# Retention attention before two expert layers: state products as 64x64 blocks, and half of the masked scores left out in tiles 4 to 11

## The chip, the cores and the metric

The kernel runs on one core of one Trainium2 chip. The metric is the device time of one execution in microseconds, as the median of several runs. A core has a matrix engine (PE, TensorE, 128 rows by 128 columns; the profile shows the loads of its weights apart as PEld), a vector engine (DVE), a scalar engine (ACT), a general engine (POOL), and queues that issue transfers (SP above all). Matmuls write into PSUM, eight banks of 128 partitions by 512 floats, which DVE and ACT read.

## The reference, cut to what matters

For each of 2 batches and 8 heads, 768 tokens of 64 features go through a decaying linear attention; its output (1536 tokens of 512 features) goes through two layers of the same form.

```
state = gamma * state + k[t] outer v[t]            # per head, 64x64
y[t] = scale * q[t] @ state
x = y as (1536, 512)
layer(x, w_in, w_out, f) = f(x @ w_in) @ w_out     # 512 -> 2048 -> 512
out = layer(layer(x, ..., elu), ..., softplus)
```

## The kernel before

The tokens are cut into 12 tiles of 128, six of a batch. Within a tile the attention is done in chunked form. With q scaled by a power of gamma and v by its inverse, a tile's output is (q times the state at the tile's start) plus (the masked 128x128 scores times v); the state then takes in the tile's k and v. All of this is float32. The layers work on blocks of 512 tokens (4 tiles) in 16 units of 128 hidden features, 96 units in all; each factor is split into a rounded part and a rest, so that each product is made of three passes.

The order of everything is a list of steps, `OPENING`, followed by what `regular()` makes of the rest; a step's name is followed by the tile's or unit's number, and each engine takes its own instructions in the order of the list. The steps that matter here:

- `Lq`, `Lk`, `Lv`, `Lw`: transfers of a tile's q, k, v and of a piece of the weights, all issued by SP.
- `dq`, `dv`: scaling of q (DVE, tiles 0 and 1) and of v (POOL). `kc.n`: n matmuls on zeros, which write nothing that is used.
- `Tq`, `Tk`: q and k turned to features by tokens, two heads at a time (L241, four matmuls); `tq` (DVE) and `tk` (ACT) copy them out. Tiles 9 to 11 are turned on DVE instead.
- `S`: scores (L300), eight matmuls with 64 rows; the two heads of a pair use the upper and the lower 64 rows and write to two banks. `m`: the mask, two operations of DVE (L310).
- `ST`, `st`: the tile's contribution to the state (L280, eight matmuls with 64 output columns, 64 wide), added and scaled on DVE.
- `sp`: POOL copies the states of two heads into the two diagonal 64x64 blocks of a 128x128 tile `wide`, whose other blocks hold zeros (L271).
- `O`: the output (`attend`). If the tile isn't a batch's first, `wide` times q for two heads at once (L322, four matmuls); then v times the masked scores (L328, eight matmuls with 128 rows and 64 output columns). `xh` (ACT) and `xl` (DVE) split the result for the layers.
- `ca`, `cb`, `ih`, `il`, `oh`, `ol`: conversion and splitting of weights. `H`, `aa`, `ab`, `gh`, `gl`, `R`, `F`: a unit's first product (L356, 12 matmuls), activation, splitting, second product (L418, 12 matmuls) and end of a block.

A float32 matmul of `S`, `ST` or `O` stands as two matmuls in the trace: the four of L322 are x8 there, the eight of L328, L300 and L280 are x16. A transpose and a matmul of the layers stand as one.

Of the kernel before, what the change touches and what calls it, by code (L numbers as in the profile page):

```python
# [37 lines left out]
def tile_retention_elu_softplus(  # L38
# [43 lines left out]
    def load(n, j):  # L82
# [24 lines left out]
    dec = const.tile([P, 2 * H + HP], F32, name="dec")  # L107
    gq = const.tile([P, HP * P], F32, name="gq")
    nc.scalar.dma_start(out=dec, in_=decay)
    gv = dec[:, 0:H].unsqueeze(2).to_broadcast([P, H, D])  # L110
    gt = dec[:, H + HP:].unsqueeze(2).to_broadcast([P, H, D])
# [9 lines left out]
                            compare_op=ALU.is_ge, fill=0.0)  # L121
    one = ones[:, 0:1]
# [5 lines left out]
    wb = ps.tile([P, 512], F32, tag="a3", name="wb")  # L128

    def keep_clock(n):  # L130
        for _ in range(n):
            nc.tensor.matmul(wb, warm[:, 0:P], warm, start=True, stop=True)  # L132
# [74 lines left out]
    def psum(tag):  # L207
        return ps.tile([P, 512], F32, tag=tag, name=tag)


    banks = ["h0", "h1", "a0", "a1", "a2", "r0", "r1"]
    turn = [0]

    def few_banks():
        banks[:] = ["r0", "r1"]
        turn[0] = 0

    def rbank():
        turn[0] += 1
        return psum(banks[(turn[0] - 1) % len(banks)])  # L220

    wide = [const.tile([P, HP, P], F32, name=f"wide{i}") for i in range(2)]
    for w in wide:
        nc.gpsimd.memset(w, 0.0)
# [399 lines left out]
```

## Time and profile before

| | |
|---|---|
| median of 3 runs | 587.7 us (587.6 to 587.92) |
| the profiled execution | 587.7 us, of which the span from its first to its last instruction is 586.0 us |
| busy: PE | 580.2 us (99%), 3012 matmuls |
| busy: DVE, ACT, POOL | 465.5, 413.3 and 30.2 us |
| granted TensorE clock | 1.0 throughout |

The time of the execution is 1.7 us more than the span; what is worked out on the span is carried over with that. Busy shares are of the whole span; a matmul's recorded duration is longer than the distance to the next one, since matmuls overlap, so the rate of PE is read from starts, not from durations.

### The profile page before, as it was taken

To read this page: it belongs to the slowest core of one execution; us is meant where nothing else is said; L and a number is where in the kernel's file an instruction comes from. 1 tells how busy PE (TensorE), PEld (TensorE's weight loads), DVE (VectorE), ACT (ScalarE), POOL (GpSimd) and SP (SyncE) were. 2 spreads that over 40 slices of the span, in tenths; PEclk is the share of its full clock that TensorE was granted. 3 is DMA by queue.
4 is the path that set the end of the run, shared out by engine and by line. 5 is a ranking of instruction groups with operands and counts; after the bars stand their busy time and mean duration, and the time that the engine had idled before them with its cause. 6 is when DMAs were issued, how large, how long until landed. Compare 5 with 4: busy or idle time off the path is not lost.

```text
span 586.0 us, 8280 instructions
## 1 busy us (share of the span) xinstructions
PE 580.2 (99%) x3012; PEld 478.3 (82%) x3012; DVE 465.5 (79%) x746; ACT 413.3 (71%) x696; POOL 30.2 (5%) x45
## 2 busy tenths in 40 slices
PE   8999999999999999999999999999999999999997
PEld 5888888888888888888888888888888888888886
DVE  4999899975664456898898998788878778878775
ACT  2688887945454557889889777767766766766763
POOL 3202010121020000000000000000000000000000
PEclk9999999999999999999999999999999999999999
DMA  9977676634310001365553000000100000100001
GB/s 222 320 202 240 205 199 201 188 103 92 66 19 1 1 0 54 101 205 157 167 179 109 0 2 0 1 0 2 72 1 0 1 0 2 72 2 1 0 1 72
DMA packets 71705, 47.74 MB, mean 81 GB/s; under 512 B 49520, under 2 KB 65904, under 8 KB 71664
## 3 DMA queue, kind: packets, MB, share of 16 engines
q1 hardware_dynamic: 71376, 46.94, 27.7%
q8 instruction: 24, 0.39, 0.3%
q10 hardware_dynamic: 288, 0.27, 0.1%
q14 instruction: 17, 0.14, 0.1%
HBM read 44.05 MB, written 3.15 MB: 81 GB/s over the span
## 4 chain that ended last, share of the span: by engine, by line
PE 98%; DMA 1%; ACT 0%; DVE 0%; issue 0%
PE h L356 45%; PE a L418 38%; PE r L418 7%; PE r L300 2%; PE r L328 2%; PE r L322 1%; PE r L280 1%; PE r L241 1%; DMA xl<-q 1%; PE h L241 0%; PE a L241 0%; PE a L300 0%; PE a L328 0%; PE a L322 0%; PE wb L132 0%; ACT kT L260 0%
## 5 line engine op out<-in xcount | busy, mean ns | idle before, releaser
L356 PE MATMUL h<-xh,wh 128*128 128x512 f32 x384 | 103.2, 391 | 0.0
L356 PE MATMUL h<-xh,wl 128*128 128x512 f32 x384 | 102.7, 389 | 0.0
L356 PE MATMUL h<-xl,wh 128*128 128x512 f32 x384 | 102.7, 389 | 0.0
L356 PEld LDWEIGHTS h<-xl,wh 128*128 128x128 f32 x384 | 72.1, 188 | 15.0
L356 PEld LDWEIGHTS h<-xh,wl 128*128 128x128 f32 x384 | 72.1, 188 | 15.1
L356 PEld LDWEIGHTS h<-xh,wh 128*128 128x128 f32 x384 | 71.7, 188 | 15.1 <-issue 0.3
L196 DVE TENSOR_TENSOR wl<-wo,wh 128x512 fp32r<-128x512 f32 x96 | 66.9, 697 | 18.4 <-ACT wh L190 18.3
L190 ACT ACTIVATE wh<-wo 128x512 fp32r<-128x512 f32 x96 | 60.3, 629 | 27.9 <-PE a L418 24.7
L196 DVE TENSOR_TENSOR wl<-wi,wh 128x512 fp32r<-128x512 f32 x96 | 66.5, 693 | 0.3 <-ACT wh L190 0.2
L190 ACT ACTIVATE wh<-wi 128x512 fp32r<-128x512 f32 x96 | 59.5, 620 | 0.7 <-DVE wi L183 0.7
L418 PE MATMUL a<-gh,wh 128*128 128x512 f32 x192 | 56.2, 399 | 0.0
L418 PE MATMUL a<-gh,wl 128*128 128x512 f32 x192 | 54.4, 390 | 0.0
L418 PE MATMUL a<-gl,wh 128*128 128x512 f32 x192 | 54.3, 389 | 0.0
L391 ACT ACTIVATE gh<-w 128x512 fp32r<-128x512 f32 x48 | 30.3, 632 | 33.9 <-DVE w L386 33.9
L370 ACT ACTIVATE e<-h 128x512 f32<-128x512 f32 x48 | 28.6, 596 | 31.7 <-PE h L356 31.7
L365 ACT ACTIVATE e<-h 128x512 f32<-128x512 f32 x48 | 28.6, 596 | 30.0 <-PE h L356 29.1
L383 DVE TENSOR_SCALAR w<-e 128x512 f32<-128x512 f32 x48 | 20.5, 426 | 36.5 <-ACT e L371 36.4
L170 ACT ACTIVATE cl<-raw,half 128x512 int32<-128x512 uint32 x64 | 48.4, 756 | 0.1
L379 DVE SCALAR_TENSOR_TENSOR e<-e,h 128x512 f32<-128x512 f32 x48 | 32.7, 680 | 18.5 <-ACT e L366 18.5
L182 DVE SCALAR_TENSOR_TENSOR cl<-cm,cl 128x512 int32<-128x512 int32 x64 | 44.9, 702 | 1.8 <-ACT cl L170 1.8
L169 ACT ACTIVATE cm<-raw 128x512 f32<-128x512 f32 x64 | 42.4, 663 | 3.2 <-DMA raw<-moe_w_out 1.5
L418 PEld LDWEIGHTS a<-gh,wl 128*128 128x128 f32 x192 | 36.1, 188 | 7.7
(124 smaller groups left out, 916.1 us busy)
## 6 DMA issues: line engine op xcount, KB each, us to landing
raw<-moe_w_in SPq DMA_DIRECT2D x32, 512.0 KB, 3.9
raw<-moe_w_out SPq DMA_DIRECT2D x32, 512.0 KB, 3.7
out_dram<-o SPq DMA_DIRECT2D x11, 256.0 KB, 2.0
k<-k SPq DMA_DIRECT2D x8, 256.0 KB, 4.3
v<-v SPq DMA_DIRECT2D x8, 256.0 KB, 4.9
q<-q SPq DMA_DIRECT2D x5, 256.0 KB, 6.0
xl<-q SPq DMA_DIRECT2D x4, 256.0 KB, 4.1
xh<-k SPq DMA_DIRECT2D x4, 256.0 KB, 3.9
```

What stands on the lines that cost most here:

```text
L169: nc.scalar.activation(out=m, in_=r[:, :, :, 1].bitcast(F32), func=AF.Copy, scale=2.0 ** -112)
L170: nc.scalar.activation(out=l, in_=r[:, :, :, 0].bitcast(U32), func=AF.Relu, scale=2.0 ** -29, bias=half)
L182: nc.vector.scalar_tensor_tensor(out=l, in0=m.bitcast(I32), scalar=3, in1=l, op0=ALU.logical_shift_left, op1=ALU.bitwise_or)
L190: nc.scalar.activation(out=h, in_=wf[f][o], func=AF.Copy)
L196: nc.vector.tensor_tensor(out=l, in0=wf[f][o], in1=ws[u, o][0].bitcast(F32), op=ALU.subtract)
L356: nc.tensor.matmul(b, w[:, kk, :], x[:, kk, :], start=(n == 0), stop=(n == len(seq) - 1))
L365: nc.scalar.activation(out=e, in_=h, func=AF.Relu, scale=-1.0)
L370: nc.scalar.activation(out=e, in_=h, func=AF.Abs)
L379: nc.vector.scalar_tensor_tensor(out=e, in0=e, scalar=-1.0, in1=h, op0=ALU.add, op1=ALU.max)
L383: nc.vector.tensor_scalar(out=w, in0=e, scalar1=1.0, scalar2=-1.0, op0=ALU.add, op1=ALU.add)
L391: nc.scalar.activation(out=gh, in_=acts[u][0], func=AF.Copy)
L418: nc.tensor.matmul(acc[i], st[:, i * P:(i + 1) * P], mv, start=(fresh and p == 0), stop=(f == NF - 1 and p == 2))
```

## The change

In `attend` the product with the state is no longer made with `wide` for two heads at once. Each head's 64x64 state is a weight block of its own, and four heads stand in the four 64x64 quadrants of the matrix engine: eight matmuls in place of four. The head's place (upper or lower 64 rows) is now `h // 4` instead of `h % 2`, and the output has its head `h % 2` in the output partitions and `h // 4` in the bank, so it takes two neighbouring banks. `sp`, `wide` and their copies go away.

In tiles 4 to 11 (`turned_tiles`) v times the masked scores is done in two parts: the first 64 queries with the first 64 values alone (64 rows, 64 output columns, 64 wide), and the last 64 queries with all 128 values (128 rows, 64 wide). To have the first 64 values of the second four heads in the lower partitions, the two halves of their tokens are exchanged when k and v are loaded, with a mask `mask_t` to match.

The eight banks of PSUM are one tile, `psb`; a bank is picked by a list in order of use, scores and outputs take pairs, and a state may take a free bank of `h`. Loads of q and k from tile 1 on are cut into two transfers, those of k and v of tiles 4 to 11 into three. `OPENING` is written anew: it is longer (up to unit 14 of the first layer), and its start has another order of loads and transposes.

```diff
-Lq.0 Lk.1 Lk.0 Lq.1 dq.0 Lv.0 Tq.0 kc.3 Lk.2 Lq.2 Tk.0 kc.2 Lv.1 Tk.1 dq.1 tk.1 Lg.0 tq.0 Tq.1 Lv.2 tk.0 dv.0 tq.1 S.0
+Lq.0 Lk.1 Lq.1 Lk.0 dq.0 Lq.2 Tq.0 kc.3 Lv.0 dq.1 Lv.1 tq.0 Lk.2 Tk.0 Tq.1 tk.0 Lq.3 tq.1 S.0 Lg.0 Lk.3 Tk.1 dv.0 m.0
+Tq.2 tk.1 Lv.2 ST.0 dv.1 Lk.4 O.0 S.1 Lw.0 xh.0 Lv.3 xl.0 kc.2 st.0 Lq.4 ST.1 m.1 Tk.2 Lw.1 tk.2 Lw.3 tq.2 O.1 Lw.2
...
-        nc.sync.dma_start(out=t, in_=src[b, :, c * P:(c + 1) * P, :].rearrange("h s d -> s h d"))
+        src = src[b, :, c * P:(c + 1) * P, :].rearrange("h s d -> s h d")
+        if n and j in turned_tiles:
+            lo, hi = (t[:, 0::2, :], t[:, 1::2, :]) if n == 1 else (t[:, :HP, :], t[:, HP:, :])
+            nc.sync.dma_start(out=lo, in_=src[:, :HP, :])
+            nc.sync.dma_start(out=hi[D:], in_=src[:D, HP:, :])
+            nc.sync.dma_start(out=hi[:D], in_=src[D:, HP:, :])
+        elif n == 2 or j == 0:
+            nc.sync.dma_start(out=t, in_=src)
+        else:
+            for i in range(2):
+                nc.sync.dma_start(out=t[:, i::2, :], in_=src[:, i * HP:(i + 1) * HP, :])
...
-    def spread_state(j):
-        if j % CPB and j < NTILE:
-            for i in range(2):
-                r = slice(i * D, (i + 1) * D)
-                nc.gpsimd.tensor_copy(wide[j % 2][r, :, r], states[j][r])
...
-        b = bank["s", j] = rbank()
...
+        free = [n for n in range(2) if n not in hbanks.values()]
+        bank["s", j] = (free[0], psb[:, free[0]]) if hbanks and free else rbank()
...
-        b = bank["o", j] = rbank()
-        first = True
-        if j % CPB:
-            s = wide[j % 2]
-            for pr in range(HP):
-                nc.tensor.matmul(b[:, pr * P:(pr + 1) * P], s[:, pr, :], qT[:, pr, :], start=(pr == 0), stop=False,
-                                 skip_group_check=True)
-            first = False
-        for pr in range(HP):
-            for i in range(2):
-                o = i * D
-                nc.tensor.matmul(b[o:o + D, pr * P:(pr + 1) * P], vt[:, 2 * pr + i, :], a[i][:, pr, :],
-                                 start=(first and pr == 0), stop=(pr == HP - 1), skip_group_check=True)
...
+        bank["o", j] = rbank(2)
+        b = bank["o", j][1]
+        inter = j % CPB > 0
+        if inter:
+            for pr in range(0, HP, 2):
+                for i in range(2):
+                    for e in range(2):
+                        r = slice(i * D, (i + 1) * D)
+                        nc.tensor.matmul(b[e * D:(e + 1) * D, i, pr * D:pr * D + P], states[j][r, pr + e, :], qT[r, pr + e, :],
+                                         start=(pr == 0), stop=False, skip_group_check=True)
+        if j in turned_tiles:
+            for o in range(0, HP, 2):
+                for i in range(2):
+                    for e in range(2):
+                        r = slice(i * D, (i + 1) * D)
+                        nc.tensor.matmul(b[e * D:(e + 1) * D, i, o * D:o * D + D], vt[r, i * HP + o + e, :], a[i][r, o + e, 0:D],
+                                         start=(not inter and o == 0), stop=False, skip_group_check=True)
+            for o in range(0, HP, 2):
+                for i in range(2):
+                    for e in range(2):
+                        nc.tensor.matmul(b[e * D:(e + 1) * D, i, o * D + D:o * D + P], vt[:, i * HP + o + e, :], a[i][:, o + e, D:P],
+                                         start=False, stop=(o > 0), skip_group_check=True)
+            return
...
```

Three places show what moves. The first is PE around the output of tile 7, between a unit's products; a row is one line's matmuls that follow each other, L322 and L328 are the output, L280 the state. Before:

```order
L356 MATMUL h_1263<-xh_293,wl 128x512 x4
L322 MATMUL r_1280<-qT,wide_146 128x128 x4
L328 MATMUL r_1280<-A,v 64x128 x8
L280 MATMUL r_1295<-v,k 64x64 x8
L418 MATMUL a_630<-gh,wh 128x512
```

In the change the same tile's output stands after the second product of a unit; L369 is the product with the states, L376 and L381 are the two parts of the masked scores, L323 is the state:

```order
L485 MATMUL psb<-gl,wh 128x512 x4
L369 MATMUL psb<-qT,st 64x128 x8
L376 MATMUL psb<-A,v 64x64 x8
L381 MATMUL psb<-A,v 64x64 x8
L323 MATMUL psb<-v,k 64x64 x8
L485 MATMUL psb<-gh,wh 128x512 x4
```

Twelve matmuls of width 128 became eight of width 128 and sixteen of width 64, in three shapes instead of two.

The second place is PE's start, from the transpose of tile 0's k on, where L132 (L155) are the matmuls on zeros. Before:

```order
L241 MATMUL h_165<-ident,xh_89 128x128 x4
L132 LDWEIGHTS warm
L132 MATMUL wb<-warm 128x512
L132 LDWEIGHTS warm
L132 MATMUL wb<-warm 128x512
L241 MATMUL a_173<-ident,xh_89 128x128 x4
L241 MATMUL a_184<-ident,xl_88 128x128 x4
L300 MATMUL a_195<-qT,kT 128x128
```

In the change (L281 are the transposes, of k with `xh`, of q with `xl`; L344 the scores, L323 the state, L388 the output of tile 0):

```order
L281 MATMUL psb<-ident,xh_89 128x128 x4
L281 MATMUL psb<-ident,xl_88 128x128 x4
L344 MATMUL psb<-qT,kT 128x128 x8
L281 MATMUL psb<-ident,xh_89 128x128 x4
L281 MATMUL psb<-ident,xl_88 128x128 x4
L323 MATMUL psb<-xl_90,xh_89 64x64 x8
L388 MATMUL psb<-A,xl_90 64x128 x8
L344 MATMUL psb<-qT,kT 128x128 x8
L155 LDWEIGHTS warm
L155 MATMUL psb<-warm 128x512
```

The transpose of k of tile 1 and two matmuls on zeros moved from ahead of the first scores to behind them.

The third place is DVE between the mask of tile 4 and the splitting that the first unit's second product (`R.0`) reads, in the change; L205 and L206 convert weights, L219 splits them, L445 is the activation and L462 its splitting:

```order
L354 TENSOR_TENSOR A<-psb,mask 128x512 x2
L205 SCALAR_TENSOR_TENSOR cl<-cm,cl 128x512
L206 SCALAR_TENSOR_TENSOR wo_117<-raw,cl 128x512
L445 SCALAR_TENSOR_TENSOR e<-e,psb 128x512
L205 SCALAR_TENSOR_TENSOR cl<-cm,cl 128x512
L206 SCALAR_TENSOR_TENSOR wi_122<-raw,cl 128x512
L219 TENSOR_TENSOR wl<-wi_120,wh 128x512
L205 SCALAR_TENSOR_TENSOR cl<-cm,cl 128x512
L206 SCALAR_TENSOR_TENSOR wo_119<-raw,cl 128x512
L219 TENSOR_TENSOR wl<-wo_117,wh 128x512
L462 TENSOR_TENSOR gl<-e,gh 128x512
```

Before, 18 operations stood in this place, and PE made the first products of units 2 and 3 ahead of a second product; now it makes that of unit 2 alone.

## Rows read from the trace of the kernel before

**Rows 1.** Page: busy us of each engine; granted clock in 40 slices, tenths.
```profile
PE 580.2 (99%) x3012; PEld 478.3 (82%) x3012; DVE 465.5 (79%) x746; ACT 413.3 (71%) x696; POOL 30.2 (5%) x45
...
PEclk9999999999999999999999999999999999999999
```
**Rows 2.** Page, the chain that ended last: share of the span by engine.
```profile
PE 98%; DMA 1%; ACT 0%; DVE 0%; issue 0%
```
**Rows 3.** Timeline of PE, tile 7: start us, us, line, tiles, shape, count.
```profile
95.14 1.07 PE L356 MATMUL h<-xh,wh 128*128 128x512 f32 x4
...
97.86 1.05 PE L322 MATMUL r<-qT,wide 128*128 128x128 f32 x8
98.84 1.09 PE L328 MATMUL r<-A,v 128*64 128x128 f32 x16
99.77 0.63 PE L280 MATMUL r<-v,k 128*64 128x64 f32 x16
100.33 1.20 PE L418 MATMUL a<-gh,wh 128*128 128x512 f32 x4
...
103.21 1.07 PE L356 MATMUL h<-xh,wh 128*128 128x512 f32 x4
```
**Rows 4.** One line's operations (L322, L328, L280): ns min/median/max, first and last start.
```profile
L322 PE MATMUL r<-qT,wide x56: 270/275/275, 33.1 to 180.6; 128*128 128x128 f32 x56
L328 PE MATMUL r<-A,v x128: 272/273/324, 34.1 to 181.6; 128*64 128x128 f32 x128
L280 PE MATMUL r<-v,k x96: 219/222/271, 41.2 to 161.9; 128*64 128x64 f32 x96
```
**Rows 5.** Timeline of PE: scores of tiles 0 and 3, matmul by matmul.
```profile
9.19 0.27 PE L300 MATMUL a<-qT,kT 64*128 64x128 f32 x1
9.19 0.27 PE L300 MATMUL r<-qT,kT 64*128 64x128 f32 x1
9.30 0.27 PE L300 MATMUL a<-qT,kT 64*128 64x128 f32 x1
...
19.93 0.27 PE L300 MATMUL h<-xh 64*128 64x128 f32 x1
19.96 0.27 PE L300 MATMUL r<-xh 64*128 64x128 f32 x1
20.04 0.27 PE L300 MATMUL h<-xh 64*128 64x128 f32 x1
```
**Rows 6.** Timeline of PE, the start, up to the first scores.
```profile
6.77 0.59 PE L132 MATMUL wb<-warm 128*128 128x512 bf16 x2
7.20 0.60 PE L241 MATMUL a<-ident,xh 128*128 128x128 f32 x4
7.64 0.66 PE L241 MATMUL a<-ident,xl 128*128 128x128 f32 x4
8.97 0.37 PE L300 MATMUL a<-qT,kT 64*128 64x128 f32 x1 [0.68 <-ACT kT L260]
```
**Rows 7.** Timelines of ACT (L260) and DVE, the same stretch.
```profile
7.84 0.60 ACT L260 ACTIVATE kT<-a 128x512 f32<-128x512 f32 x1 [5.75 <-PE a L241]
8.33 0.59 ACT L260 ACTIVATE kT<-h 128x512 f32<-128x512 f32 x1
...
6.89 0.69 DVE L231 TENSOR_TENSOR xl<-xl,dec 128x512 f32<-128x512 f32 x1 [2.41 <-DMA xl<-q]
```
**Rows 8.** Windows: busy us of each engine (count), clock, DMA share, GB/s.
```profile
25.80:58.00 32.20, 32.20 (x195) 26.22 (x194) 30.94 (x49) 28.22 (x49) 4.94 (x5) 1.00 0.78 234
58.00:98.00 40.00, 40.00 (x246) 32.79 (x245) 37.68 (x61) 35.74 (x63) 2.64 (x3) 1.00 0.71 211
```
**Rows 9.** Timeline of DVE, weights converted and split, one after the other.
```profile
23.58 0.68 DVE L182 SCALAR_TENSOR_TENSOR cl<-cm,cl 128x512 int32<-128x512 int32 x1
24.29 0.69 DVE L183 SCALAR_TENSOR_TENSOR wi<-raw,cl 128x512 int32<-128x512 int32 x1
24.90 0.68 DVE L339 TENSOR_TENSOR xl<-h,xh 128x512 fp32r<-128x512 f32 x1
25.50 0.68 DVE L196 TENSOR_TENSOR wl<-wi,wh 128x512 fp32r<-128x512 f32 x1
```

More of the change, by code (lines that the diff above doesn't have):

```diff
@@ L121, in tile_retention_elu_softplus @@
                             compare_op=ALU.is_ge, fill=0.0)
+    mask_t = const.tile([P, P], F32, name="mask_t")
+    for i in range(2):
+        nc.gpsimd.affine_select(out=mask_t[i * D:(i + 1) * D], in_=ones[i * D:(i + 1) * D], pattern=[[1, P]], base=(i - 1) * D,
+                                channel_multiplier=-1, compare_op=ALU.is_ge, fill=0.0)
     one = ones[:, 0:1]
@@ L127, in tile_retention_elu_softplus @@
     nc.vector.memset(warm, 0.0)
[L128 removed]
+    psb = ps.tile([P, 8, 512], F32, name="psb")
+    names = ("h0", "h1", "a0", "a1", "a2", "a3", "r0", "r1")
     def keep_clock(n):
         for _ in range(n):
[L132 removed]
+            nc.tensor.matmul(psb[:, 5], warm[:, 0:P], warm, start=True, stop=True)
     keep_clock(7)
@@ L207, in psum, with rbank, keep, release @@
     def psum(tag):
[L208 to L224, printed above, removed]
+        n = names.index(tag)
+        assert n not in live
+        return psb[:, n]
+    banks = [2, 3, 4, 6, 7, 0, 1, 5]
+    live = set()
+    def rbank(n=1):
+        free = [b for b in banks if b not in live]
+        if n == 2:
+            b = min((p for p in (0, 2, 4, 6) if p in free and p + 1 in free), key=lambda p: max(free.index(p), free.index(p + 1)))
+        else:
+            b = free[0]
+        for i in range(b, b + n):
+            banks.remove(i)
+            banks.append(i)
+            live.add(i)
+        return b, psb[:, b] if n == 1 else psb[:, b:b + 2]
+    def keep(n):
+        keep_clock(n)
+        banks.remove(5)
+        banks.append(5)
+    def release(key):
+        b, t = bank.pop(key)
+        live.discard(b)
+        if key[0] in "ao":
+            live.discard(b + 1)
+        return t
     qkT = {}
@@ L309, in causal @@
         for i in range(2):
-            nc.vector.tensor_tensor(out=a[i], in0=bs[i].rearrange("p (h t) -> p h t", h=HP),
-                                    in1=mask.unsqueeze(1).to_broadcast([P, HP, P]), op=ALU.mult)
+            nc.vector.tensor_tensor(out=a[i], in0=bs[:, i].rearrange("p (h t) -> p h t", h=HP),
+                                    in1=(mask_t if i and j in turned_tiles else mask).unsqueeze(1).to_broadcast([P, HP, P]), op=ALU.mult)
         scores[j] = a
@@ new lines, in attend, with turned, feature @@
+        for n in range(H):
+            i, pr = (n % 2, n // 2) if j == 0 else divmod(n, HP)
+            h = head(j, i, pr)
+            e, o = h % 2, h % HP // 2 * P
+            nc.tensor.matmul(b[e * D:(e + 1) * D, h // HP, o:o + P], vt[:, h, :], a[i][:, pr, :], start=(not inter and h % HP < 2),
+                             stop=(h % HP >= 2), skip_group_check=True)
+    def turned(b):
+        return b[:, :, 0:2 * P].rearrange("p i (a t) -> p i a t", a=2)
+    def feature(x, j):
+        return x[:, :, (j % TPB) * P:(j % TPB + 1) * P].rearrange("p (i a) t -> p i a t", i=2)
@@ L352, in hidden @@
         b = psum(f"h{u % 2}")
+        banks[:] = [n for n in banks if n > 1]
+        hbanks[u] = u % 2
         passes = [(ah, xh), (ah, xl), (al, xh)] if u else [(ah, xh), (al, xh), (ah, xl)]
@@ L376, in act_b @@
         h = hb.pop(u)
+        del hbanks[u]
         e = acts[u][0]
@@ L405, in project @@
             opened.add((layer, blk))
+            banks[:] = [n for n in banks if n > 5]
             for i in range(4):
```

99 lines of the change are left out of this document (57 added, 42 removed).

## The prediction

> **What bounds the kernel now.** I read the page's busy times first, then the chain of waits, and then PE's timeline, because the first two leave only one engine to look at. PE is busy 99% of the span, at full clock throughout [rows 1], and the chain that ended last lies on PE for 98% [rows 2]. So a microsecond less on PE is a microsecond less in the end, as long as nothing else becomes late. Everything the change touches lies in the first third of the span: the last output of a tile starts before 182 us [rows 4].
>
> The reader is to see three things in PE's timeline. The first is the step. L322 has eight matmuls in 1.05 us, of which the last takes 0.275, so one starts each (1.05 - 0.275) / 7 = 0.111 us [rows 3, 4]. The scores also take 0.11 a step, but two start in each: at 9.19 one into bank a and one into r, and again at 9.30 [rows 5]. They sit in different halves of the array and run side by side. L328 and L280, whose outputs have 64 columns, do the same: 16 matmuls of L328 take 0.93 us, which is eight steps of 0.11 and a little, and in L280, 64 wide, a step is (0.63 - 0.222) / 7 = 0.058 us [rows 3, 4]. The second is that the two halves keep their own time: in tile 3 bank h starts at 19.93 and 20.04, bank r between them at 19.96, each 0.11 after its last [rows 5]. The third is that a change of shape costs. L322 takes 0.98 us for 0.89 of steps and L328 0.93 for 0.88, so to enter the 64-column shape costs about 0.14; L280 takes 0.56 for 0.46, and the 12 matmuls after it 2.88 where 12 undisturbed ones take 2.72, so to leave it for the full shape costs 0.26 [rows 3]. A way in and out is 0.40.
>
> **The change, part by part.**
>
> *State product.* L322 has eight steps of 0.111 in each of ten tiles. In quadrants there are 16 matmuls, and if four run side by side that is four steps: 4 x 0.11 less in each tile, 4.4 us in all. No row shows 64 rows and 64 columns at once. Bounds: if only two run side by side there are eight steps and nothing is saved; four give 4.4. I take 4.4, since halves by rows [rows 5] and halves by columns [rows 3] each run at full pace, the rows' halves keep their own time, and the two halves by rows write to different banks here as they do in the scores.
>
> *Half of the masked scores.* In each of eight tiles eight steps of 0.11 (0.88) become 16 matmuls in quadrants, four steps of 0.058, and 16 of 64 columns, eight steps of 0.058: 0.70 in all. Saved: 8 x 0.18 = 1.4 us. The uncertain part is the first. Four matmuls in 0.058 us is one each 15 ns, and the densest stretch of before is L280's two in 0.058, one each 29 ns [rows 3, 4]. If 29 ns is what PE can do, the 16 take 0.46 instead of 0.23, and this edit loses 0.4 instead of gaining 1.4. I take the 1.4, because two matmuls of L300 stand within 0.01 of each other [rows 5], so 29 ns is not the least distance between two starts.
>
> The Trainium skill has a rule that speaks against this: in TensorE: Matmul & The Clock Gate, section "Wait — 56ns, not 53.3ns?", it says that the distance from start to start never falls below about 25 ns, however narrow the matmul. The starts within 0.01 us of each other in the two halves disagree with it for matmuls in different parts of the array [rows 5]; for a mean over many no row here decides. By the rule the 16 would take 0.40 and the edit would save next to nothing (an estimate from that page).
>
> *Changes of shape.* I count them in the two orders of PE: 49 before, 63 after. Those into or out of the full shape go from 44 to 46; those between two part shapes (quadrants to columns above all, within each output) go from 5 to 17. Of the added 12, at the price of entering the 64-column shape, 12 x 0.14 = 1.7; of the 2, at half a way in and out, 0.4. Together 2.1 us more. The bounds are 0.09 and 0.26 each [rows 3], so 1.3 to 3.6.
>
> *Sum on PE:* 4.4 + 1.4 - 2.1 = 3.7 us less.
>
> *The start.* The first scores wait for ACT's second copy of a turned k: it stands behind that of tile 1 and runs from 8.33, and the scores start at 8.97 after 0.68 idle [rows 6, 7]. In the change k of tile 0 is turned and copied alone. It is now the fourth tile in SP's queue; the fourth of before was q of tile 1, and the operation that waited for it started at 6.89 [rows 7]. From a transpose's start to ACT's copy is 7.84 - 7.20 = 0.64, the copy takes 0.60: 6.89 + 1.24 gives scores at about 8.15, 0.8 earlier. But two matmuls on zeros (7.20 - 6.77 = 0.43) and one transpose (0.44) [rows 6] now stand behind the scores, where PE no longer waits: 0.9 later. Net 0.1 more. The loads cut in two carry the same bytes; if they cost SP more, the 0.8 shrinks, and if the matmuls on zeros fill a wait, 0.4 comes back. I keep 0.4 either way.
>
> *What is late next.* DVE does the same work as before, and where PE is to run ahead it has little room: busy 30.94 of 32.20 us, then 37.68 of 40.00 [rows 8]. Third place of the order: from the mask of tile 4 to the splitting that R.0's third matmul reads DVE has two masks, an activation and two splits before the last at 0.60 each, three conversions at 0.71 + 0.61, and 0.68 for the last [rows 9]: 3.0 + 4.0 + 0.7 = 7.7 us after the scores of tile 4. PE has in that time two first products (2 x 2.88 [rows 3], next to changes of shape) and an output (16 steps, 1.13, and three changes), about 7.3, and R.0's third matmul two starts later, at 7.8. So it is in time only if DVE isn't behind when tile 4's scores end; behind the waiting matmul stand all of R.0 and the units after it. Before, two more units of PE work covered that. I take 0.4 us for new waits of this sort, and 0 to 1.2 as bounds (1.2 is what the change saves on PE in the 72 us of these windows, three tiles at 0.4).
>
> *POOL.* Its copies (`sp`) go, and nothing waits for what takes their place: the state is read by PE straight from DVE's tile. It saves nothing, since no wait of PE stood on them.
>
> *Total:* -3.7 + 0.1 + 0.4 = -3.2 us. The profiled span of 586.0 becomes 582.8, and with the same 1.7 around it the time goes from 587.7, which is also the median, to 584.5.
>
> **The rivals.**
>
> *A. A floor on starts.* Quadrants overlap, but PE starts no more than one matmul each 29 ns. The state product, 16 x 0.029 = 0.46 against 0.44, hardly feels it; the first half of the scores loses 0.23 in eight tiles, 1.9 us. Time 586.4. For it: no denser stretch is in the trace. Against it: starts 0.01 apart [rows 5]. By the skill's 25 ns, named above, the loss is 1.4 and the time 585.9.
>
> *B. Quadrants don't run four at a time.* Two of them still do. Then the state product saves nothing (4.4 lost) and the first half of the scores takes eight steps, 0.23 more in eight tiles (1.9 lost): 584.5 + 6.3 = 590.8, slower. It decides from one point on: with the state product at eight steps, the added changes of shape (2.1) outweigh all that the halved scores can bring (1.4). For it: no row has both halvings at once. Against it: each alone works at full pace, and the two halves by rows aren't held in step [rows 5].
>
> *C. DVE eats it.* The new order leaves PE waiting in the first 98 us by 1.2 to 1.8 more than I took: time 585.7 to 586.3. For it: 96% and 94% [rows 8]. Against it: there is no wait of PE in those windows before, with 3.6 us of DVE's time idle.
>
> **How the numbers follow.** My forecast has a chance of 0.60, A 0.18, C 0.12, B 0.10. The prediction is the forecast's, 584.5. Its own ends: with changes of shape at 0.09 and no new waits 587.7 - 5.8 + 1.3 + 0.1 = 583.3, with those at 0.26 and the waits 586.0. The range is 583.0 to 586.6: below, it allows 0.3 for the matmuls on zeros filling a wait; above, it takes in A and C and leaves out B. A change of 0.2% (1.2 us, to 586.5 or 588.9) is about the least that a measurement of this kernel can tell from none. The forecast is faster by more; A, at 586.4, sits on the bound and is split evenly; C is faster in two of three; B is slower. That makes 0.77 faster, 0.13 the same and 0.10 slower.
>
> **What would show it.** Right: between the product before and the state after a tile's output, L369 takes about 0.5 us, L376 0.25 to 0.35 and L381 0.5; starts of L369 come in fours each 0.11; between 182 us and the end nothing differs but the offset. The first scores start near 8.15. Wrong by A: L376 takes 0.5 or more. Wrong by B: L369 takes 0.95. Wrong by C: PE has idle rows with DVE as their releaser before 98 us, at R.0 first. What I would least expect is a first wait on SP: its queue has three transfers per k and v of tiles 4 to 11 where it had one.

## The result, and the profile after

The changed kernel takes 591.13 us (median of four runs, 590.38 to 591.78) where the kernel before takes 587.81 (four runs, 587.60 to 587.98): ratio 1.0057, 95% interval 1.0042 to 1.0072. The profiled execution takes 590.86 us, its span 589.1, against 586.0 before. It is slower by 3.3 us where 3.2 less were forecast.

The page of the changed kernel, its lines of busy time and of the chain that ended last (they answer to [rows 1, 2]):

```profile
PE 578.5 (98%) x3219; PEld 472.4 (80%) x3220; DVE 465.5 (79%) x746; ACT 413.3 (70%) x696; POOL 20.0 (3%) x25
...
PE 88%; SPq 6%; DMA 3%; DVE 1%; issue 1%; ACT 1%; DVEq 0%
```

PE has less to do (578.5 us where [rows 1] have 580.2) and is idle more: 10.6 us of the span instead of 5.8, and SP's queue and the DMA engines, which had 1% of the chain, now have 9%. So the question is not whether PE's work shrank but what it waits for.

Its timeline around tile 7's output (for [rows 3]):

```profile
100.66 0.67 PE L369 MATMUL psb<-qT,st 64*64 64x128 f32 x16
101.15 0.41 PE L376 MATMUL psb<-A,v 64*64 64x64 f32 x16
101.49 0.69 PE L381 MATMUL psb<-A,v 128*64 128x64 f32 x16
102.01 0.64 PE L323 MATMUL psb<-v,k 128*64 128x64 f32 x16
102.57 0.73 PE L485 MATMUL psb<-gh,wh 128*128 128x512 f32 x2
```

and its operations by line (ns min/median/max, first and last start; for [rows 4]):

```profile
L369 PE MATMUL psb<-qT,st x128: 269/269/321, 16.5 to 183.9; 64*64 64x128 f32 x128
...
L376 PE MATMUL psb<-A,v x128: 216/218/267, 35.9 to 184.1; 64*64 64x64 f32 x128
```

The reader is to see that the quadrants work as forecast. L369 takes 0.49 us to the next line; its 16 matmuls last 0.67 of which the last is 0.269, so one starts each (0.67 - 0.269) / 15 = 0.027 us, four in 0.11. L376 takes 0.34, one start each (0.41 - 0.218) / 15 = 0.013 us. From L369 to the product after it this tile takes 1.91 us; before it took 2.47 [rows 3]. The two edits can be told apart on the output of tile 9, from its first matmul to the state after it: 1.91 us before, 1.52 in f3 (an experiment below, with the state product in quadrants and whole scores there), 1.34 in the changed kernel.

The other places hold the loss. The start, on PE (for [rows 6]), and ACT's first copy of a turned k (for [rows 7]):

```profile
5.05 1.09 PE L281 MATMUL psb<-ident,xl 128*128 128x128 f32 x4 [0.63 <-DVE xl L270]
5.93 1.49 PE L155 MATMUL psb<-warm 128*128 128x512 bf16 x3
7.81 1.11 PE L281 MATMUL psb<-ident,xh 128*128 128x128 f32 x4 [0.40 <-DMA xh<-k]
8.72 1.02 PE L281 MATMUL psb<-ident,xl 128*128 128x128 f32 x4
9.67 1.16 PE L344 MATMUL psb<-qT,kT 64*128 64x128 f32 x16
```

```profile
8.96 0.60 ACT L300 ACTIVATE kT<-psb 128x512 f32<-128x512 f32 x1 [6.88 <-PE psb L281]
```

The first scores start at 9.67, not at 8.15: the transposition of k waits for its load until 7.81, and from there to ACT's copy it takes 1.15 us, not 0.64. PE is still slow there: a transposition's matmul starts 0.213 us after the last one, and 0.109 once PE is fast. The trace's record of the granted clock begins at 9.56 us, at full; in the kernel before it begins at 5.85. (Windows print 1.00 for the time ahead of it too, where nothing is recorded.) Then, before the first H, O.3 waits for DVE; here is PE, and DVE in the same stretch:

```profile
24.18 0.66 PE L281 MATMUL psb<-ident,k 128*128 128x128 f32 x4
26.02 0.67 PE L369 MATMUL psb<-xh,st 64*64 64x128 f32 x16 [1.19 <-DVE xl L403]
...
28.41 0.97 PE L421 MATMUL psb<-xh,wh 128*128 128x512 f32 x3
```

```profile
21.99 1.45 DVE L205 SCALAR_TENSOR_TENSOR cl<-cm,cl 128x512 int32<-128x512 int32 x1
23.48 0.69 DVE L206 SCALAR_TENSOR_TENSOR wi<-raw,cl 128x512 int32<-128x512 int32 x1
24.09 1.28 DVE L354 TENSOR_TENSOR A<-psb,mask 128x512 f32<-128x512 f32 x2
25.29 1.28 DVE L403 TENSOR_TENSOR xl<-psb,xh 128x512 fp32r<-128x512 f32 x2
```

An output now writes a pair of banks, and O.3 gets the pair of O.1, which L403 (`xl.1`) frees; in the new list that step stands behind a weight conversion and a mask. Last, the scores of tiles 10 and 11 on PE, and the queue of SP ahead of the first of them:

```profile
155.24 1.16 PE L344 MATMUL psb<-qT,kT 64*128 64x128 f32 x16 [1.05 <-DVE kT L288]
...
176.70 1.16 PE L344 MATMUL psb<-qT,kT 64*128 64x128 f32 x16 [1.62 <-DVE kT L288]
```

```profile
131.17 0.61 SPq L100 DMA_DIRECT2D k<-k  x1
131.83 0.77 SPq L101 DMA_DIRECT2D k<-k  x1
132.70 0.55 SPq L99 DMA_DIRECT2D v<-v  x1
133.29 1.67 SPq L100 DMA_DIRECT2D v<-v  x1
135.01 0.70 SPq L101 DMA_DIRECT2D v<-v  x1
135.81 8.98 SPq L120 DMA_DIRECT2D qb<-q  x16
145.21 7.43 SPq L120 DMA_DIRECT2D qb<-k  x16
```

SP issues the six pieces of tile 10's k and v, then the 32 pieces of its q and k in blocks until 152.6, and PE's scores come 2.6 later.

How far each kernel is behind the one before, in us, at points where both have done the same work (starts in PE's timelines; R.12 is the second product of the 13th unit; the last four columns are experiments, below):

```
             before   changed   d1     f1     f3     g3
scores.0       8.97    +0.70  +0.35  -0.29  -1.14  -0.54
first H       25.76    +2.65  +1.45  +0.73  -0.03  +1.18
R.12         121.49    +1.75  +1.45  +0.75  +0.58  +2.45
R.16         147.35    +1.23  +1.45  +0.43  +0.26  +2.12
R.20         174.24    +3.55  +1.45  +0.14  +0.26  +2.47
R.22         187.41    +3.06  +1.45  -0.16  -0.04  +2.16
```

Read down the column of the changed kernel: 2.65 late at the first H, then gaining, 0.52 in the one tile between R.12 and R.16, then tiles 10 and 11 take it back, and from R.22 to the end nothing changes. PE's timeline gives both sides of it. The outputs O.1 to O.3 take 4.9 us where they took 6.1, so the opening lost not 2.65 but 2.65 + 1.3 = 3.9. From the first H on, R.0 waits 0.6 (in the first three gaps between its starts) and the scores of tiles 10 and 11 wait 2.7, together 3.3, and the kernel falls back by only 3.06 - 2.65 = 0.4: so PE gained 2.9 there (the outputs O.4 to O.11 take 10.7 us in place of 14.6; some of that is given back around them). In all PE saves 1.3 + 2.9 = 4.2 us, and 3.9 + 3.3 = 7.2 are lost. The 3.3 are waits. Of the 3.9, waits are 1.9: PE idles 4.04 us before the first H and idled 2.14. About 1.4 more are pace (an estimate): PE has 7.28 us of work ahead of the record's begin at full clock, before it had 4.40, and half of the difference would have been saved at the full clock.

### The profile page after: what moved, and what is told of

Its sections match the earlier page's. It is cut to its first block, busy times and chain, and to the rows that moved or that the text cites. A ratio compares the mean times of both kernels' runs of the same rounds, so it can differ in the third digit from the quotient of the medians.

```text
span 589.1 us, 8710 instructions
## 1 busy us (share of the span) xinstructions
PE 578.5 (98%) x3219; PEld 472.4 (80%) x3220; DVE 465.5 (79%) x746; ACT 413.3 (70%) x696; POOL 20.0 (3%) x25
## 4 chain that ended last, share of the span: by engine, by line
PE 88%; SPq 6%; DMA 3%; DVE 1%; issue 1%; ACT 1%; DVEq 0%
PE psb L485 43%; PE psb L421 41%; SPq L120 2%; SPq L106 1%; DMA raw<-moe_w_in 1%; PE psb L344 1%; PE psb L381 1%; SPq L103 1%; PE psb L369 1%; SPq L183 1%; DMA qb<-k 1%; PE psb L281 1%; DMA q<-q 1%; PE psb L323 0%; SPq L99 0%
## 5 line engine op out<-in xcount | busy, mean ns | idle before, releaser
L421 PE MATMUL psb<-xh,wh 128*128 128x512 f32 x384 | 103.9, 392 | 0.1
L421 PE MATMUL psb<-xl,wh 128*128 128x512 f32 x384 | 102.7, 389 | 0.0
L421 PE MATMUL psb<-xh,wl 128*128 128x512 f32 x384 | 102.7, 389 | 0.0
L421 PEld LDWEIGHTS psb<-xl,wh 128*128 128x128 f32 x384 | 72.1, 188 | 15.2
L421 PEld LDWEIGHTS psb<-xh,wl 128*128 128x128 f32 x384 | 72.1, 188 | 15.0
L421 PEld LDWEIGHTS psb<-xh,wh 128*128 128x128 f32 x384 | 71.2, 188 | 15.1 <-ACT xh L399 0.4
L219 DVE TENSOR_TENSOR wl<-wo,wh 128x512 fp32r<-128x512 f32 x96 | 66.4, 693 | 14.6 <-ACT wh L213 14.5
L219 DVE TENSOR_TENSOR wl<-wi,wh 128x512 fp32r<-128x512 f32 x96 | 65.9, 686 | 0.0
L485 PE MATMUL psb<-gh,wh 128*128 128x512 f32 x192 | 55.9, 398 | 0.0
L485 PE MATMUL psb<-gl,wh 128*128 128x512 f32 x192 | 54.4, 390 | 0.1
L485 PE MATMUL psb<-gh,wl 128*128 128x512 f32 x192 | 54.5, 390 | 0.0
L435 ACT ACTIVATE e<-psb 128x512 f32<-128x512 f32 x48 | 28.6, 597 | 32.1 <-PE psb L421 32.1
L430 ACT ACTIVATE e<-psb 128x512 f32<-128x512 f32 x48 | 28.5, 593 | 30.1 <-PE psb L421 30.0
L205 DVE SCALAR_TENSOR_TENSOR cl<-cm,cl 128x512 int32<-128x512 int32 x64 | 45.2, 707 | 2.5 <-ACT cl L193 2.3
```

Of the source, the lines that this page charges most:

```text
L205: nc.vector.scalar_tensor_tensor(out=l, in0=m.bitcast(I32), scalar=3, in1=l, op0=ALU.logical_shift_left, op1=ALU.bitwise_or)
L219: nc.vector.tensor_tensor(out=l, in0=wf[f][o], in1=ws[u, o][0].bitcast(F32), op=ALU.subtract)
L421: nc.tensor.matmul(b, w[:, kk, :], x[:, kk, :], start=(n == 0), stop=(n == len(seq) - 1))
L430: nc.scalar.activation(out=e, in_=h, func=AF.Relu, scale=-1.0)
L435: nc.scalar.activation(out=e, in_=h, func=AF.Abs)
L485: nc.tensor.matmul(acc[i], st[:, i * P:(i + 1) * P], mv, start=(fresh and p == 0), stop=(f == NF - 1 and p == 2))
```

## The experiments

All were timed in five rounds against the kernel before on the same chip; not all groups ran on one chip, and the kernel before took 587.93 to 588.20 us on them. Theory 1 blamed the cutting of the loads; rival 2 the order of the steps; rival 3 the gaps between the pieces that are written.

**a1 and a2: the kernel before with loads cut.**

```
+ for i in range(2):            # a1: q of tiles 1 to 8, k of 1 to 3
+     nc.sync.dma_start(out=t[:, i*HP:(i+1)*HP, :], in_=src[:, i*HP:(i+1)*HP, :])
+ nc.sync.dma_start(out=t[:, :HP, :], in_=src[:, :HP, :])      # a2: k, v of 4 to 11
+ nc.sync.dma_start(out=t[D:, HP:, :], in_=src[D:, HP:, :])
+ nc.sync.dma_start(out=t[:D, HP:, :], in_=src[:D, HP:, :])
```

> The kernel before, with q of tiles 1 to 8 and k of tiles 1 to 3 loaded in two transfers each of four heads (the same bytes to the same places, no other change). Theory 1 (cut transfers cost): in the changed kernel two halves take about 1.2 us where a whole one took 0.9 to 1.05, so eight to ten loads of the opening come 1 to 2 us later in sum, the first scores some 0.3 to 0.7 us later and the first H 1 to 2.5 us later: 588.8 to 590.3. Rival 2 (the new order of the opening is what costs, not the cutting): 587.5 to 588.1. Rival 3 (the cost is in the interleaved places that the halves are written to, not in their number): 587.5 to 588.1 too, since here each half is written in one piece per partition.

> The kernel before, with k and v of tiles 4 to 11 loaded in three transfers each (the same bytes to the same places, no other change). Theory 1 (SP's queue is full with issues when the loads in blocks of tiles 10 and 11 are due): PE waits about 1 us before the scores of tile 10 and 1 to 1.7 us before those of tile 11, with SP's queue in the chain there, and nothing changes before 100 us: 589.5 to 590.8. Rival 2 (the order of the steps, or the interleaved places, makes these scores late): no wait there, 587.5 to 588.2.

a1: 588.52 us, ratio 1.0007 (0.9998 to 1.0015); a2: 588.39, 1.0005 (0.9996 to 1.0014). Both are within the error of no change, and in a2 PE doesn't wait before the scores of tiles 10 and 11, which start at 153.85 and 174.12. Theory 1 falls as it was stated: cutting alone costs at most 0.9 us.

**b4: the changed kernel with whole loads, c1: with fewer cut ones.**

```
- nc.tensor.transpose(b[:, pr*P:(pr+1)*P], x[:, 2*pr:2*pr+2, :]..., ident)   # b4
+ for i in range(2):
+     nc.tensor.matmul(b[i*D:(i+1)*D, pr*P:(pr+1)*P], x[:, i*HP+pr, :], ident, ...)
- turned_tiles = range(TPB, NTILE)                                           # c1
+ turned_tiles = range(TPB, DVE_TILES)
```

> The changed kernel with every load as whole as before, in natural order of the heads (each transposition is done by two matmuls of 64 columns against the identity in place of one of 128), and without the half scores (whole masked scores in all tiles); the order of the steps is that of the changed kernel. Theory 1: the state product's gain of 4.4 stays, the 1.4 of the half scores is left out, 2.1 of changed shapes stays, both load waits go, the late DVE at the first R (0.55) stays: 586.0, between 585.3 and 587.0, first scores near 8.2 us, no wait before the scores of tiles 10 and 11. Rival 2 (order): the opening keeps some 3 us: 588.5 to 589.5, first scores near 9.5 us.

> The changed kernel with half scores in tiles 4 to 8 only; tiles 9 to 11 (whose q and k come in blocks too) have whole scores, k in two transfers and v in one. Theory 1 (SP's issues): the waits before the scores of tiles 10 and 11 (1.13 and 1.69 us) go, three tiles lose the 0.17 us of half scores each, and the opening stays as it is: 588.5 to 589.2. Rival 2 (these scores are late by the order or by DVE's own work): the waits stay and 0.5 comes on top: 591.2 to 591.8.

b4: 597.40 us, 1.0161 (1.0147 to 1.0175); its transposing matmuls keep PE busy for 589.4 us (581.7 in d4, below, which differs by them, by the cuts and by 64 bytes of shift), so its time tells nothing of the loads. Its trace does: the DMA engines brought whole loads no faster (windows 5 to 20 us: share 1.25 at 231 GB/s), and the first scores start at 11.15. Neither theory expected that. c1: 592.41, 1.0079 (1.0066 to 1.0093). The waits before the scores of tiles 10 and 11 shrink from 1.05 and 1.62 us to 0.68 and none, as theory 1 has it, and yet the kernel is no faster. Its start shows where the time goes, on PE:

```profile
9.86 2.08 PE L344 MATMUL psb<-qT,kT 64*128 64x128 f32 x16
11.87 1.11 PE L281 MATMUL psb<-ident,xh 128*128 128x128 f32 x4
12.78 0.98 PE L281 MATMUL psb<-ident,xl 128*128 128x128 f32 x4
```

The first scores take 2.01 us to the next line, in the changed kernel 1.09, and each four transpositions after them 0.9 instead of 0.5. This is the pace of the lower of PE's two levels (1.2 GHz); the record of the granted clock begins, at full, at 13.55 us. PE had idled 0.76 us ahead of the first transposition and 0.42 ahead of the next, where before idles 0.20. That the pauses are the reason isn't shown: e3 (below) idles 0.77 and 0.26 in the same places, and its record begins at 4.75.

**d1 to d4: the addresses.** b4 pointed at something that whole and cut loads share. The change's table of decays takes 144 bytes of each partition in place of 80, which moves all later tiles by 64 bytes (what else came or went is a multiple of 256 bytes long). The theory is that before has its tiles on multiples of 256; no trace records an address, so the runs can show only what a shift does.

```
- dec = const.tile([P, 2*H+HP], F32, name="dec")
+ dec = const.tile([P, 2*H+HP+16], F32, name="dec")   # d1; d2 to d4: 4*H+HP+16
```

> The kernel before with 16 unused columns behind the decays, so that every tile behind them (all that q, k, v and the weights are loaded to) starts 64 bytes later, off the multiples of 128 bytes where before has them; nothing else is changed. A new theory 4: the changed kernel's larger table of decays moved all tiles to 64 past a multiple of 128, and it is this, not the cutting of transfers, that lets the DMA engines of the opening bring 220 GB/s (5 to 20 us) where before brings 254. Theory 4: this kernel brings about 220 there, its first scores come 0.5 to 1.5 us later than at 8.97, and its first H 1 to 2.5 us later: 588.8 to 590.3. Theory 1 (cut transfers) and rival 2 (order): 254 as before and 587.5 to 588.3.

> The changed kernel with 16 unused columns behind the decays, so that every tile behind them starts on a multiple of 128 bytes again, as in the kernel before; nothing else is changed. Theory 4 (addresses): the opening's transfers come at 250 GB/s or more, its first scores near 8.5 us in place of 9.67, the first H near 26 in place of 28.4, and the waits before the scores of tiles 10 and 11 shrink with the time that SP's issues take: 586.0 to 588.5. Theory 1 (cut transfers) and rival 2 (order): 590.5 to 591.8, as the changed kernel.

> The same, and half scores in tiles 4 to 8 only; tiles 9 to 11 have whole scores, with k in two transfers and v in one. If theory 4 is right and SP's issues alone make the scores of tiles 10 and 11 late, this is faster than the last one by what is left of these waits (0 to 2.8 us) less 0.5 us of half scores: 585.0 to 586.5. If the addresses cause both, it is 0.5 us slower than the last one.

> The changed kernel with every tile on a multiple of 128 bytes, and without the half scores: whole masked scores in all tiles, q and k in two transfers, v in one. Theory 4: the opening as in the last two; the state product in quadrants keeps its 4.4 us less 2.1 of changed shapes, no wait before the scores of tiles 10 and 11: 585.5 to 587.0. Half scores are then worth the difference to the one before, 0.17 us for each of five tiles. Theory 1: the opening stays late, 588.5 to 590.

d1: 589.28 us, 1.0021 (1.0013 to 1.0030), every run slower than the median of before. The windows from 5 to 20 us (the last two numbers are the DMA share and GB/s) of before, the changed kernel and d1:

```profile
5.00:20.00 15.00, 14.32 (x197) 12.29 (x197) 10.17 (x18) 3.82 (x7) 6.50 (x10) 1.00 1.06 254
```
```profile
5.00:20.00 15.00, 14.09 (x163) 11.05 (x165) 7.54 (x14) 2.49 (x5) 3.13 (x3) 1.00 1.20 220
```
```profile
5.00:20.00 15.00, 13.93 (x173) 11.35 (x173) 9.37 (x17) 2.93 (x6) 5.32 (x8) 1.00 1.25 216
```

The share per 100 GB/s, 0.42 before, is 0.55 in the changed kernel and 0.58 in d1: for the same bytes the packets' times add up to a third more. Shares over 1 mean that these times overlap, so the loss of speed is smaller: SP's second to seventh load, 256 KB each, land 1.20 us apart in d1, 1.04 in the mean before. But d2 (593.36 us, 1.0081), d3 (590.61, 1.0043) and d4 (591.36, 1.0052) did not get it back: their tiles are shifted by 128 bytes against before, and d2's share per 100 GB/s is 0.53.

**e1 to e3: other shifts.** e1 and e2 are the changed kernel and c1 with 112 unused columns (448 bytes, with the 64 a shift of 512); e3 is before with 32 (128 bytes).

> The changed kernel with 112 unused columns behind the decays, so that every tile behind them starts on a multiple of 256 bytes (as in the kernel before; the pieces that the q, k and v loads write are 256 bytes each); the changed kernel has them 64 past one, and the last attempt 128 past one; nothing else is changed. Theory 4 in this form (a piece that crosses a multiple of 256 bytes costs the DMA engines more): a 256 KB load of the opening takes 0.9 to 1.0 us in place of 1.20, first scores at 8.2 to 8.8 us in place of 9.67, first H near 26 in place of 28.4, and the waits before the scores of tiles 10 and 11 shrink or go: 584.5 to 588. Rival 3 (it is the writing with gaps between the pieces that takes 1.20 us per 256 KB): the opening stays, 590 to 593.5.

> The same with half scores in tiles 4 to 8 only (whole scores in tiles 9 to 11, k in two transfers and v in one). Theory 4: as the last one if no wait is left before the scores of tiles 10 and 11 there (then 0.5 us slower), faster than it by what is left of these waits less 0.5 otherwise: 584.5 to 586.5. Rival 3: 589.5 to 592.

> The kernel before with 32 unused columns behind its decays: every tile starts 128 past a multiple of 256 bytes, nothing else is changed. The shift by 64 cost 1.1 us, with 1.20 us for each 256 KB load. Theory 4 with 256 bytes: the same again, 588.8 to 590, loads of 1.2 us. With multiples of 128 bytes as what counts: 587.7 to 588.5, loads of 0.9 to 1.0.

e3: 589.50 us, 1.0024 (1.0014 to 1.0034), as slow as d1: a shift by 128 costs what one by 64 does. e1's window:

```profile
5.00:20.00 15.00, 13.01 (x181) 10.29 (x180) 8.33 (x15) 2.98 (x5) 3.13 (x3) 1.00 0.95 225
```

0.42 again, and its first scores start at 8.87. Rival 3 falls: with the gaps between the pieces still there, the packets take no longer than before. That multiples of 256 are enough, and not only those of 512, no run shows. Yet e1 takes 590.69 us, 1.0047 (1.0035 to 1.0059), hardly less than the changed kernel, and e2 590.47, 1.0038 (1.0026 to 1.0050), although in e2 no wait is left before the scores of tiles 10 and 11. In both, O.3 waits longer, in e2 1.77 us; it starts at 25.69 and 25.57 whatever the scores do. So there is a second cause behind the first.

**f1 to f4: what O.3 waits for, and the clock.** f1 and f2 are e2 with one edit each, f3 has both and a third; f1 and f3 also name each step's bank as e2 had it, so that the moved steps alone differ. f4 is the changed kernel with nine matmuls on zeros at the very start (`keep_clock`) in place of seven.

```
- O.1 Lw.2 st.1 Lk.5 ... xh.2 xh.1 ST.3 m.3 ... tk.4 xl.1 ca.1 xl.2 O.3
+ O.1 xh.1 Lw.2 st.1 xl.1 Lk.5 ... xh.2 ST.3 m.3 ... tk.4 ca.1 xl.2 O.3      # f1, f3
- Lq.0 Lk.1 Lq.1 Lk.0          keep_clock(7)
+ Lq.0 Lk.0 Lq.1 Lk.1          keep_clock(8)                                 # f2, f3
- dv.1 Lk.4 O.0 S.1 Lw.0 xh.0 Lv.3
+ dv.1 Lw.0 O.0 S.1 Lv.3 xh.0 Lk.4                                           # f3
```

> The last but one (tiles on multiples of 256 bytes, half scores in tiles 4 to 8) with two steps of the opening moved: the rounding of tile 1's attended values (xh.1 on ACT, xl.1 on DVE) right behind O.1, in place of behind the first weight conversion and the masked scores of tile 3; the banks are pinned to those of before the move. In that kernel O.3 waits 1.9 us (from 23.5 to 25.57) for xl.1, which frees its two banks. Theory 5 (a new wait of this order: O takes a pair of banks, and DVE frees it behind the conversion of the first weights): O.3 starts near 24.3, the first H near 26.8 in place of 27.96, 588.8 to 589.6 in median. Rival 6 (DVE's queue as a whole bounds the stretch to 60 us, so that only the place of the wait moves): O.3 earlier, but the first R as late as before, 590.0 to 590.6.

> The same kernel without that move, but with k of tile 0 loaded second (before k of tile 1 and q of tile 1) and eight bf16 matmuls ahead of the first transposition in place of seven. The transposition of k waits for its load until 7.28 us there. Theory 2b (the new order of loads makes the first scores late): first scores near 7.6 in place of 8.63; if O.3 waits for DVE as theory 5 has it, it starts at 25.5 all the same and the time stays within 0.4 us of 590.5. If the first scores set the end: 589.5.

> Both moves, and the first weights' load ahead of k and v of tiles 4 and 3. Theory 5 and 2b together: first scores near 7.6, first weights 1.5 us earlier than at 20.4, O.3 near 23.5, first H near 25.8 to 26.3: 587.5 to 588.6, about the kernel before. Rival 6: 589.5 to 590.5.

> The changed kernel with nine bf16 matmuls ahead of its first transposition in place of seven, nothing else. Theory 7 (TensorE idles 0.63 us ahead of the first transposition, where before idles 0.20, and then runs the next transpositions, in other runs also the first scores and two more groups of transpositions, at half speed): with no pause there all transpositions from 7.8 us on take 0.11 each, the first scores come 0.5 to 0.9 us earlier, and the times lie closer together: 590.0 to 590.6, spread under 1 us. Without an effect of the pause: 590.8 to 591.8, spread 1.4 us or more.

f1: 588.50 us, 1.0009 (1.0001 to 1.0018), 2.0 less than e2 (1.7 by the two ratios to before). PE's timeline:

```profile
23.20 0.66 PE L284 MATMUL psb<-ident,k 128*128 128x128 f32 x4
23.79 0.67 PE L372 MATMUL psb<-xh,st 64*64 64x128 f32 x16
24.38 1.09 PE L391 MATMUL psb<-A,xl 128*64 128x128 f32 x16
25.41 0.66 PE L284 MATMUL psb<-ident,q 128*128 128x128 f32 x4
26.49 0.72 PE L424 MATMUL psb<-xh,wh 128*128 128x512 f32 x2 [0.42 <-ACT xh L402]
```

The wait is gone and the first H 1.5 earlier: theory 5 holds, and rival 6 falls for this wait. f2: 589.43, 1.0027 (1.0017 to 1.0037), first scores at 8.04, O.3 at 24.84 with its wait: 1.0 less than e2, more than theory 5 allowed. f3: 587.18 us, 0.9990 (0.9982 to 0.9999), the first to be faster than before, if barely.

f3's profiled execution took 588.52 us, the longest of its eleven, so its rows aren't those of its median. They show one more loss, at the very end. The last output's transfer lands 2.79 us after its issue, 2.06 before, and one packet of an instruction queue (8 KB, 0.76 us) lies among its packets. So it is in the traces of all nine kernels with half scores in tiles 4 to 8 alone (landing after 2.59 to 2.80 us) and in none of the eleven others (2.04 to 2.13). Therefore f1, f3 and g3 end 0.7 to 0.8 us later than their last row in the table says. Why the packet falls there wasn't asked.

f4 contradicts theory 7: 592.77 us, 1.0070 (1.0048 to 1.0092), times from 590.09 to 594.63. The first scores come 0.4 earlier than in the changed kernel, but here the clock falls later. Windows of PE: busy us, granted clock, DMA share, GB/s.

```profile
24.00:26.00 2.00, 0.52 (x4) 1.00 1.04 391
26.00:27.00 1.00, 0.79 (x20) 1.00 1.10 318
27.00:28.00 1.00, 1.00 (x16) 0.63 1.28 236
28.00:29.00 1.00, 1.00 (x7) 0.50 1.11 261
29.00:30.00 1.00, 1.00 (x5) 0.50 1.08 287
30.00:31.00 1.00, 1.00 (x4) 0.66 0.57 129
```

After 1.69 us of idling before O.3, and about a microsecond of work, the clock is granted at half (1.2 GHz) for some 3.4 us, and about 1.7 are lost. The runs differ accordingly: the two at a mean clock of 1.000 take 590.1 and 590.4 us, three at 0.997 take 592.7 to 592.9, the one at 0.994 takes 594.6. Of the 52 runs of the eight experiments in which O.3 waits 0.77 us or more (c1, d2 to d4, e1, e2, f2, f4) 24 have a mean clock below 0.998; of the 49 runs of f1, f3 and the three below, without it, none. Some of the eight have other long waits too, but f2 has not, and 4 of its 12 runs are among the 24. So the wait costs twice, itself and now and then a half-speed stretch; this is also why medians of these kernels can't tell half a microsecond. In the changed kernel's own four runs the clock was 0.999 or 1.000.

**g1 to g3: what is left.** g1 is f3 with `Lw.1` ahead of `Lk.4 Lq.4` and `Lw.2` ahead of `Lw.3`; g2 is g1 without `kc.2`; g3 is f3 without the unused columns.

> The fastest kernel so far (tiles on multiples of 256 bytes, half scores in tiles 4 to 8, xl.1 early, k of tile 0 second, first weights early; 587.18) with the second weights' load ahead of k and q of tile 4 and the third ahead of the fourth. There H.1 waits 0.53 us beyond its scores for wh, the second weights having landed at about 27.2. If the loads' order still sets the end of the opening: H.1 0.5 to 0.8 earlier, 586.4 to 586.9. If DVE's queue does (rival 6): the first R waits as long or longer, 587.0 to 587.5.

> The same without the two bf16 matmuls behind the scores of tile 1 (0.52 us of TensorE and the wait for the bank that they write, 0.39). If TensorE's own order sets the opening: another 0.5 to 0.9 earlier, 585.7 to 586.5. If loads or DVE set it: within 0.3 of the last one.

> The kernel with 587.18 us without the unused columns, so that its tiles start 64 past a multiple of 256 bytes as in the changed kernel. The shift cost the kernel before 1.1 and 1.4 us, and taking it from the changed kernel gave nothing that could be told while O.3 waited for DVE. If the addresses count where the opening is bound by loads: 588.2 to 589.0. If not: 587.0 to 587.6.

g1: 587.21 us, 0.9989 (0.9980 to 0.9998); g2: 587.29, 0.9991 (0.9982 to 1.0000): neither move is worth anything that can be told. g3: 590.59, 1.0041 (1.0029 to 1.0054): 3.4 us for 64 bytes, more than in d1 and more than expected; why it is more isn't shown.

## Why the prediction was wrong

*The state product: right.* 0.49 us in place of 0.98; rival B, two at a time, is refuted, and that the time came out near its 590.8 is chance. *Half of the masked scores: right.* One start each 0.013 us, so rival A's 0.029 doesn't hold, and tile 9's output is shorter by 1.52 - 1.34 = 0.18, the forecast's 0.18. The Trainium skill has a least distance of about 25 ns between starts (TensorE: Matmul & The Clock Gate, section "Wait — 56ns, not 53.3ns?"). Between quadrants it doesn't hold either; within one quadrant a start comes each 0.051 us. *Changes of shape, and the sum of 3.7:* the accounting above gives 4.2, and 0.52 for a tile with both edits, so they cost rather less than the 2.1 taken.

*The start: the step that failed.* "Net 0.1 more" was 3.9 by the first H; of the 6.3 us between the forecast and the profiled span this is 3.8, the waits below are 2.9, and PE's larger saving takes 0.5 off. "The loads cut in two carry the same bytes; if they cost SP more, the 0.8 shrinks" put the risk in the wrong place. Cutting costs nothing that can be told (a1). What cost was not in the working at all: the tiles' addresses (d1, e3, g3), O.3's wait for a pair of banks (f1), and PE's pace in the first microseconds, where the working took the rows of a PE already fast. The prediction followed the order of the list at the first scores and at R.0, and nowhere between; O.3 stood there with its releaser behind two steps of DVE. With addresses, order and that wait mended, and half scores left out of tiles 9 to 11, first scores come at 7.84 and the first H is no later than before (f3).

On the addresses the Trainium skill has a rule, DMA: Bandwidth & Descriptors, section "How a descriptor splits into AXI transactions": a transaction that reads starts at a multiple of 256 bytes, and a descriptor that starts elsewhere takes more beats. For 256 bytes at 64 past one it gives 10 beats in place of 8, and at 128 past one 12 (an estimate from that page). Here the side that is written is the one shifted, of which the rule doesn't speak. The runs fit a boundary of this sort, as far as shifts of 64, 128 and 512 can show it; of the sizes, d1 and e3 (0.58 and 0.56 against 0.42) show no difference between 64 and 128.

*New waits, 0.4: too small.* R.0 waits 0.6, for DVE's `wl` and `gl`, as rival C has it; C's sign, an idle row of PE with DVE as its releaser, had come before that, at O.3, with 1.19. C's larger claim, that DVE eats what PE saves, isn't settled. f3's trace starts the first H level with before and is 0.58 behind at R.12, where PE's savings should have put it ahead. There PE waits 0.53 for ACT's `wh` at H.1 and 0.50 for DVE's `wl` in R.0; but it is f3's longest run, and g1, whose trace is 0.16 ahead of before at R.12, has the same median.

*SP: "What I would least expect."* It came, 1.05 and 1.62 us. With less cutting c1 has 0.68 and none of it, e2 none; a2 shows that the pieces alone don't make it, and e1 that fast loads don't remove it (1.29 and 0.57 us). How much each of order, pieces and lateness has of it stays open, and in medians its worth isn't resolved (c1 1.3 slower than the changed kernel, d3 2.8 faster than d2, e2 0.2 faster than e1), the less so as c1, d3 and e2 have the late last transfer, 0.5 to 0.7 us.

Open too is why f3 gains only 0.6 to 0.8 us of PE's 3.7 (4.2 less the half scores of three tiles). The late last transfer takes 0.7 in its trace; the waits up to R.12 were not taken away one by one.

## What to carry to other kernels

A saving on the busiest engine is safe only if the order around it is walked through at every step that takes or frees a buffer, not at the first and last alone. Look at what a diff does to the addresses of tiles it doesn't name: a table 64 bytes longer cost 1.1 us in one kernel here (d1) and 3.4 in another (g3). And when a mended cause doesn't bring the time back, look for the wait that takes its place; here three lay behind one another.

## What the runs showed of the hardware

- Loads in pieces of 256 bytes, into tiles shifted by 64 or by 128 bytes, alike: the packets' times per byte add up to about a third more (between 5 and 20 us 0.53 to 0.58 of share per 100 GB/s in all ten traces with such a shift, 0.40 to 0.44 in the ten without, those with a shift of 512 among them), and loads of 256 KB land 1.20 us apart in place of 1.04 (d1).
- In four quadrants one matmul starts 0.013 us after the last with 64 columns and 0.027 with 128, on average over 16.
- In f4 PE idled 1.69 us and worked for about one; then the granted clock was at half from 27.3 to 30.7 us though PE was busy. In the first microseconds the record of the clock begins, at full, anywhere from 4.2 (e2) to 13.8 us (d2), and until then PE starts its matmuls half as often.
- A packet of 8 KB of an instruction queue, 0.56 to 0.76 us long, lies among the packets of the last output in nine kernels; that output lands 2.59 to 2.80 us after its issue, in the eleven others 2.04 to 2.13.
